# One weight-conversion chunk per unit in the second and third expert blocks, and two operand differences made separately

## The chip, the cores and the metric

The kernel runs on one core of a Trainium2 chip. The metric is device time in microseconds (us) of one execution. The core has a matrix engine (TensorE, "PE" in the profile, with its weight loads shown apart as "PEld"), a vector engine (VectorE, "DVE"), a scalar engine (ScalarE, "ACT"), a further elementwise engine (GpSimd, "POOL") and a sync engine (SyncE, "SP") whose queue issues every DMA of this kernel. Each engine carries out its own instructions in the order in which the program wrote them; semaphores hold an instruction back until what it reads has been written and what it overwrites has been read.

## What is computed

Three stages follow each other, all in float32. The first is windowed attention over 4 batches, 8 heads, 576 positions and 64 dimensions a head. The second routes its 2304 token rows of 512 values through all eight experts and mixes the results with a matrix `P` that is balanced by eight rounds of row and column normalisation. The third is a feed-forward layer with a cosine in it, whose two weight matrices arrive as float64 and are turned into float32 on the chip.

```python
x = attention(q, k, v)                      # (2304, 512)
for e in range(8):
    h = np.maximum(x @ w1[e], 0.0)          # (2304, 1024)
    out += P[:, e:e + 1] * (h @ w2[e])      # (2304, 512)
h = out @ w_in                              # w_in, w_out: float64
return ((h * np.cos(h)) @ w_out).astype(np.float32)
```

## The kernel before, in words

**Blocks and units.** After attention the 2304 token rows are handled as three blocks of 768 rows. The outer list `phases` is expert block 0, 1, 2 (`("moe", b)`), then feed-forward block 0, 1, 2 (`("ffn", b)`). Inside a block the kernel walks over units; a unit is a slice of 256 hidden columns. An expert block has 32 units (8 experts of 4 slices), a feed-forward block has 8, so there are 120 units. Below, "unit 8 of expert block 1" means `u == 8` there.

**The first product, `g1`.** The hidden slice (256 columns by 768 rows, split two by two) is made with seven products of half size in place of eight, in the order `ORDER = (1, 2, 6, 5, 7, 4, 3)`. Their right-hand operands are `B11, B21, T2, T1, T3, T4, B22`: three are quarters of the block's input `src`, and four are differences, `T1 = b12 - b11`, `T2 = b22 - T1`, `T3 = b22 - b12`, `T4 = b21 - T2`. Every operand is split into a rounded high part and a rest, so each product is six matmuls (L750), 42 in a unit. ACT copies partial results out of PSUM (`keep`, L773), DVE adds (L776), and ACT and DVE make the split of the ReLU (L711, L712).

**The second product, `g2`.** For each of six groups of 128 rows, six matmuls (L846 to L848) multiply the hidden slice with the second weight; DVE scales and adds the result (L837; L827 in the feed-forward blocks). The groups of a unit are carried out during the next unit, in an expert block one after each of its products two to seven, so that a unit has 42 + 36 = 78 matmuls.

**Slots and background lists.** After each product, and again after each `g2` group, the main loop calls `slot()`, which lets the first generator of each of the lists `pre`, `feed`, `bg` and `bg2` run on to its next `yield`. An expert unit therefore has 7 + 6 = 13 slots. The order in which instructions are written there is the order in which the engines take them.

**Weight conversion.** `convert_f64(c)` is on the list `bg`. It turns one of 32 chunks (128 by 512 values) of the float64 weights into float32 with seven DVE instructions (L218 to L238), one to a slot; in its eighth slot it issues the load of the next chunk's raw words (`load_f64`, L203 or L209, 512 KB, into the only tile `u0`), and in its tenth the 256 KB store of its own result (L246). The load has to wait until L234 has read the raw words of the chunk before. The result tile `fb` is single too: L230 of the next chunk waits until the store has landed. All 32 generators are appended at once, after unit 0 of expert block 1, so that a new chunk starts in the eleventh slot after the one before.

**Other background work.** `prep_ffn` (list `bg2`) starts after every fifth unit of expert blocks 1 and 2, eight times in all: it loads four converted chunks (L88), makes four differences on POOL (L120), splits eleven pieces on ACT and POOL (L179, L181) and stores them (L175). The weights of the coming units are loaded by `load_w` (L109): 1792 KB for the first product (`wa`), issued at the start of a unit, and 1024 KB for the second (`wb`), issued after the last `g2` group, when the tile that it overwrites has been read. All of these loads and stores go through SP in program order.

**Change of block.** Four units before the end of a block, `feed` starts making the next block's differences: `stages` writes `T1` and `T2` on POOL (L267); for a feed-forward block `x2_pieces` first transposes the expert result. In the last unit `combos` splits one operand after each product from the second on (ACT L284, then DVE L285). `T3` and `T4` have no tiles of their own: `T3` is written over `T1` and `T4` over `T2`, both by the callback `st["rest"]`, which runs after the split of `T1`. The tiles of `T1` and `T2` come from `u_pool` for the expert blocks and feed-forward block 0, and from `rawp` for feed-forward blocks 1 and 2. `rawp` has two buffers for each tag.

Of the kernel before, what the change touches and what calls it, by code (L numbers as in the profile page):

```python
# [29 lines left out]
def tile_attention_moe_cos_ffn(ctx, tc, q, k, v, w_gate, w1, w2, w_in, w_out, out):  # L30
# [9 lines left out]
    NU1 = E * UPE  # L40
    NU2 = DFF // FU
# [29 lines left out]
    with tc.manual_schedule():  # L71
# [123 lines left out]
        def load_f64(c):  # L195
            if c >= 4 * NU2:
                return
            s, x = divmod(c, 4)
            raw = u_pool.tile([P, 512, 2], I32, tag="u0", name=f"f64_{c}")
            if x < 2:  # L200
                for y in range(2):
                    kc = 2 * x + y
                    nc.sync.dma_start(  # L203
                        out=raw[:, y * FU:(y + 1) * FU, :].rearrange("p n t -> p (n t)"),
                        in_=w_in[kc * P:(kc + 1) * P, 2 * s * FU:2 * (s + 1) * FU],
                    )
            else:
                r0 = s * FU + (x - 2) * P
                nc.sync.dma_start(out=raw.rearrange("p n t -> p (n t)"), in_=w_out[r0:r0 + P, :])  # L209
            f64_t[c] = raw  # L210

        def convert_f64(c):
            raw = f64_t.pop(c)
            lo, hi = raw[:, :, 0], raw[:, :, 1]
            a = u_pool.tile([P, 512], I32, tag="u1", name=f"fa{c}")
            b = u_pool.tile([P, 512], I32, tag="u2", name=f"fb{c}")
            w = b.bitcast(F32)
            nc.vector.tensor_scalar(  # L218
                out=a, in0=hi, scalar1=20, scalar2=0x7FF, op0=ALU.logical_shift_right, op1=ALU.bitwise_and
            )  # L220
            yield
            nc.vector.tensor_scalar(out=a, in0=a, scalar1=896.0, scalar2=896.0, op0=ALU.max, op1=ALU.subtract)
            yield
            nc.vector.tensor_scalar(out=a, in0=a, scalar1=23, scalar2=None, op0=ALU.logical_shift_left)
            yield
            nc.vector.scalar_tensor_tensor(
                out=a, in0=hi, scalar=-2147483648, in1=a, op0=ALU.bitwise_and, op1=ALU.bitwise_or
            )
            yield
            nc.vector.tensor_scalar(  # L230
                out=b, in0=hi, scalar1=0xFFFFF, scalar2=0x100000, op0=ALU.bitwise_and, op1=ALU.bitwise_or
            )
            yield
            nc.vector.scalar_tensor_tensor(  # L234
                out=w, in0=lo.bitcast(U32), scalar=2.0 ** -32, in1=b, op0=ALU.mult, op1=ALU.add
            )
            yield
            nc.vector.scalar_tensor_tensor(  # L238
                out=w, in0=w, scalar=2.0 ** -20, in1=a.bitcast(F32), op0=ALU.mult, op1=ALU.mult
            )  # L240
            yield
            load_f64(c + 1)
            yield
            yield
            w32[c] = dram.tile([P, 512], F32, tag=f"w32_{c}", name=f"w32_{c}")
            nc.sync.dma_start(out=w32[c], in_=w)  # L246
# [6 lines left out]
        def stages(b, src):  # L253
            b11, b12 = src[:, 0:2, :HB], src[:, 0:2, HB:]
            b21, b22 = src[:, 2:4, :HB], src[:, 2:4, HB:]
            st = {}
            stg[b] = st

            def stage(nm, i, x, y, over=None):
                if over:  # L260
                    t = st[over]
                elif b in (("ffn", 1), ("ffn", 2)):
                    t = rawp.tile([P, 4, P, 2], F32, tag=("ra", "rb")[i], name=f"st{nm}_{b[0]}{b[1]}")
                    t = t.rearrange("p a f c -> p (a f c)")[:, :TB].rearrange("p (k f) -> p k f", k=2)
                else:
                    t = u_pool.tile([P, 2, HB], F32, tag=("u1", "u2")[i], name=f"st{nm}_{b[0]}{b[1]}")
                nc.gpsimd.tensor_tensor(out=t, in0=x, in1=y, op=ALU.subtract)  # L267
                st[nm] = t

            stage("T1", 0, b12, b11)  # L270
            yield
            yield
            stage("T2", 1, b22, st["T1"])
            st["rest"] = lambda: (stage("T3", 0, b22, b12, "T1"), stage("T4", 1, b21, st["T2"], "T2"))
            yield

        def combos(b, src):
            st = stg[b]
            b11, b21, b22 = src[:, 0:2, :HB], src[:, 2:4, :HB], src[:, 2:4, HB:]
            for nm in ("B11", "B21", "T2", "T1", "T3", "T4", "B22"):  # L280
                s = {"B11": b11, "B21": b21, "B22": b22}.get(nm)
                s = st[nm] if s is None else s
                t = xtp.tile([P, 2, 2, HB], F32R, tag=f"xt{nm}", name=f"xt{nm}_{b[0]}{b[1]}")
                nc.scalar.activation(out=t[:, 0], in_=s, func=AF.Copy)  # L284
                nc.vector.tensor_tensor(out=t[:, 1], in0=s, in1=t[:, 0].bitcast(F32), op=ALU.subtract)  # L285
                xt[b, nm] = t
                if nm == "T1":
                    st["rest"]()
                yield


# [310 lines left out]
        for n in range(NGR + 6):  # L602
            if n < NGR:
                pi, u = groups[n]
# [35 lines left out]
            if n == 46:  # L640
                early.append(stages(("moe", 0), xr[0]))
            if n == 54:
                early.append(combos(("moe", 0), xr[0]))
# [37 lines left out]
        bg, bg2, pre, feed = [], [], [], []  # L681

        def step_all(lst):
            if lst and next(lst[0], StopIteration) is StopIteration:
                lst.pop(0)

        def lazy(f):
            yield from f()

        def slot():  # L690
            step_all(pre)
            step_all(feed)
            step_all(bg)
            step_all(bg2)
# [163 lines left out]
        def begin(n):  # L858
            if n < len(steps):
                kind, b, u = steps[n]  # L860
                if b or kind == "ffn":
                    load_w(u, b, "a")
                elif u >= 2:
                    pre.append(prep_a(u))
            if n + 1 < len(steps):
                kind, b, u = steps[n + 1]
                if not b and kind == "moe" and u >= 3:
                    pre.append(prep_s(u))
# [10 lines left out]
        def tick():  # L879
            tail[:] = [t for t in tail if next(t, StopIteration) is not StopIteration]  # L880

        bg.append(sinkhorn((p_m, "m"), skp))
        load_f64(0)
        queue = []
        for n, s in enumerate(steps):
            kind, b, u = s
            pre += pre_next
            pre_next.clear()
            begin(n + 1)
            ph = phases.index((kind, b))  # L890
            last = n + 1 == len(steps) or steps[n + 1][:2] != (kind, b)
            nxt = phases[ph + 1] if ph + 1 < len(phases) else None
            to_end = (NU1 if kind == "moe" else NU1 + NU2) - u
            if nxt and to_end == 4:
                if nxt[0] == "ffn":
                    feed.append(x2_pieces(nxt[1]))
                    feed.append(lazy(lambda nxt=nxt: stages(nxt, x2r[nxt[1]])))
                else:
                    feed.append(stages(nxt, xr[nxt[1]]))
            nx = None  # L900
            if last and nxt:
                while feed:
                    step_all(feed)
                nx = combos(nxt, xr[nxt[1]] if nxt[0] == "moe" else x2r[nxt[1]])
            for j, _ in enumerate(g1(s)):
                tick()
                slot()
                if queue and (queue[0][0] < n - 1 or j >= (1 if steps[queue[0][0]][0] == "moe" else 6)):
                    m, tt = queue.pop(0)
                    g2(steps[m], tt)  # L910
                    if tt == TPB - 1:
                        begin_b(m + 2)
                    slot()
                tick()
                if nx and j >= 1:
                    next(nx, None)
            if nx:
                for _ in nx:
                    pass
            queue += [(n, tt) for tt in range(TPB)]  # L920
            if (kind, b) == ("moe", 1) and u == 0:
                bg += [convert_f64(c) for c in range(4 * NU2)]
            at = n - NU1
            if 0 < at <= 5 * NU2 and at % 5 == 0:
                bg2.append(prep_ffn(NU1 + at // 5 - 1))
            while pre:
                step_all(pre)
# [34 lines left out]
```

## Time and profile before

| what | value |
|---|---|
| median of three runs | 2156.83 us (2154.12 to 2157.45) |
| the profiled execution's own time | 2155.78 us |
| its span, first to last instruction | 2154.0 us |
| PE busy | 2084.9 us, 97% |
| DVE busy | 1351.5 us, 63% |
| ACT busy | 771.0 us, 36% |
| POOL busy | 470.1 us, 22% |
| moved by DMA | 456.95 MB, 212 GB/s in the mean |

An engine's busy time is the sum of the stretches in which it carried out an instruction. A matmul's end is modelled and matmuls overlap each other, so the 97% of PE does not say that it works at its peak; what a unit takes from its first matmul to the next unit's first is the better measure. In the answers about groups and in the order of time, a text in square brackets tells how long the engine stood idle before an instruction and which event ended that.

### The profile page before, as it was taken

The numbers are of one execution on the slowest core, as the hardware profiler recorded it, in microseconds if no ns is written. First come the engines' busy times: TensorE is split into PE (matmuls) and PEld (weight loads), VectorE is DVE, ScalarE is ACT, GpSimd is POOL, SyncE is SP. The second block draws the span as 40 slices with busy tenths as digits, with TensorE's granted clock in tenths as the row PEclk, the third lists the DMA queues.
The fourth block names the chain that finished last, engine by engine and source line by source line (L and its number), as shares of the span: only waits on it lengthen the run. The fifth ranks groups of instructions, "written<-read, shape, count | busy, mean of one in ns | idle before, by whom it ended". The sixth has DMA issues, their size and how long they took to land. (4 is left out here: it accounts for less than half of the span.)

```text
span 2154.0 us, 28332 instructions
## 1 busy us (share of the span) xinstructions
PE 2084.9 (97%) x10623; PEld 1816.9 (84%) x10623; DVE 1351.5 (63%) x2473; ACT 771.0 (36%) x1544; POOL 470.1 (22%) x524
## 2 busy tenths in 40 slices
PE   8989999999999989999999999999999999999998
PEld 6667888988888878777878888888989888888897
DVE  5665766666666667766775554545555466766766
ACT  6775333333333212222222232222222245454543
POOL 4343232333332001112112121110000012222222
PEclk9999999999999999999999999999999999999999
DMA  5633566676767567777786566574544444454543
GB/s 144 158 104 93 185 256 257 249 263 238 264 235 265 205 239 274 259 254 277 258 288 244 213 226 246 212 265 162 201 175 186 190 175 182 161 209 194 194 166 117
DMA packets 162105, 456.95 MB, mean 212 GB/s; under 512 B 67504, under 2 KB 106416, under 8 KB 131248
## 3 DMA queue, kind: packets, MB, share of 16 engines
q1 hardware_dynamic: 161968, 455.15, 58.3%
q8 instruction: 83, 1.36, 0.3%
q14 instruction: 54, 0.44, 0.1%
HBM read 326.65 MB, written 128.45 MB: 211 GB/s over the span
## 5 line engine op out<-in xcount | busy, mean ns | idle before, releaser
L837 DVE SCALAR_TENSOR_TENSOR acc_moe<-g_moe,prob,acc_moe 128x512 f32<-128x512 f32 x546 | 407.8, 747 | 259.3 <-PE g_moe L848 258.5
L846 PE MATMUL g_moe<-wb,h_moe 128*128 128x512 f32 x1152 | 451.9, 392 | 18.4 <-ACT h_moe L711 18.1
L848 PE MATMUL g_moe<-wb,h_moe 128*128 128x512 f32 x1152 | 461.0, 400 | 5.3 <-DVE h_moe L712 5.2
L847 PE MATMUL g_moe<-wb,h_moe 128*128 128x512 f32 x1152 | 456.2, 396 | 0.0
L773 ACT ACTIVATE s_moe<-y_moe 128x384 f32<-128x384 f32 x288 | 141.3, 491 | 682.2 <-PE y_moe L750 682.1
L750 PE MATMUL y_moe<-xtT_moe,wa 128*128 128x384 f32 x1728 | 349.8, 337 | 0.6 <-ACT s_moe L773 0.6
L750 PEld LDWEIGHTS y_moe<-xtT_moe,wa 128*128 128x128 f32 x1728 | 310.5, 189 | 26.4 <-ACT s_moe L773 0.9
L848 PEld LDWEIGHTS g_moe<-wb,h_moe 128*128 128x128 f32 x1152 | 216.6, 188 | 60.4 <-DVE h_moe L712 15.0
L711 ACT ACTIVATE h_moe<-c_moe 128x384 fp32r<-128x384 f32 x192 | 131.7, 686 | 378.7 <-DVE c_moe L776 378.7
L846 PEld LDWEIGHTS g_moe<-wb,h_moe 128*128 128x128 f32 x1152 | 217.4, 189 | 50.4 <-ACT h_moe L711 24.1
L847 PEld LDWEIGHTS g_moe<-wb,h_moe 128*128 128x128 f32 x1152 | 216.7, 188 | 27.1
L712 DVE SCALAR_TENSOR_TENSOR h_moe<-c_moe,h_moe 128x384 fp32r<-128x384 f32 x192 | 146.5, 763 | 144.5 <-ACT h_moe L711 144.5
L120 POOL TENSOR_TENSOR s<-ra 128x256 f32<-128x256 f32 x80 | 59.5, 743 | 717.0 <-DMA ra<-w 401.8
L776 DVE TENSOR_TENSOR c_moe<-z_moe,s_moe 128x384 f32<-128x384 f32 x192 | 106.6, 555 | 75.0 <-ACT s_moe L773 63.9
L738 POOL TENSOR_TENSOR h_ffn<-c_ffn,h_ffn 128x768 fp32r<-128x768 f32 x48 | 89.1, 1859 | 285.6 <-ACT h_ffn L736 220.2
L750 PE MATMUL z_moe<-xtB_moe,wa 128*128 128x384 f32 x576 | 119.1, 342 | 11.5 <-DVE c_moe L776 11.5
L750 PEld LDWEIGHTS z_moe<-xtB_moe,wa 128*128 128x128 f32 x576 | 103.5, 191 | 23.9 <-DVE c_moe L776 16.5
L750 PE MATMUL y_moe<-xtB_moe,wa 128*128 128x384 f32 x576 | 116.1, 336 | 0.0
L750 PE MATMUL z_moe<-xtT_moe,wa 128*128 128x384 f32 x576 | 115.9, 335 | 0.0
L750 PE MATMUL x_moe<-xtB_moe,wa 128*128 128x384 f32 x576 | 115.6, 335 | 0.0
L846 PE MATMUL g_ffn<-wb,h_ffn 128*128 128x512 f32 x288 | 113.0, 392 | 2.3 <-DVE acc_ffn L827 2.3
L827 DVE TENSOR_TENSOR acc_ffn<-g_ffn,acc_ffn 128x512 f32<-128x512 f32 x126 | 86.4, 687 | 44.7 <-PE g_ffn L848 43.4
(159 smaller groups left out, 3072.0 us busy)
## 6 DMA issues: line engine op xcount, KB each, us to landing
wa<-wd SPq DMA_DIRECT2D x88, 1792.0 KB, 9.1
wb<-wd SPq DMA_DIRECT2D x88, 1024.0 KB, 4.8
wd<-wa SPq DMA_DIRECT2D x32, 1792.0 KB, 6.8
wd<-wb SPq DMA_DIRECT2D x32, 1024.0 KB, 5.3
ra<-in_moe_w_dram SPq DMA_DIRECT2D x64, 256.0 KB, 7.4
rb<-in_moe_w_dram SPq DMA_DIRECT2D x64, 256.0 KB, 5.7
wd<-hla SPq DMA_DIRECT2D x48, 256.0 KB, 9.6
wd<-hlb SPq DMA_DIRECT2D x40, 256.0 KB, 7.4
```

What stands on the lines that cost most here:

```text
L120: nc.gpsimd.tensor_tensor(out=s4[:, o], in0=x, in1=y, op=op)
L711: nc.scalar.activation(out=h[:, 0, cols], in_=c, func=AF.Relu)
L712: nc.vector.scalar_tensor_tensor(out=h[:, 1, cols], in0=c, scalar=0.0, in1=h[:, 0, cols].bitcast(F32), op0=ALU.max, op1=ALU.subtract,)
L738: nc.gpsimd.tensor_tensor(out=h[:, 1], in0=c, in1=h[:, 0].bitcast(F32), op=ALU.subtract)
L750: nc.tensor.matmul(ps[:, :HB], wa[:, wl, WI[m], kc, :], x[:, xl, kc, :], start=start and kc == 0 and n_ == 0, stop=stop and kc == 1 and n_ ...
L773: nc.scalar.activation(out=snap[i], in_=y[:, :HB], func=AF.Copy)
L776: nc.vector.tensor_tensor(out=o, in0=ps[:, :HB], in1=snap[i], op=ALU.add)
L827: nc.vector.tensor_tensor(out=a, in0=ps, in1=a, op=ALU.add)
L837: nc.vector.scalar_tensor_tensor(out=a, in0=ps, scalar=pe, in1=a, op0=ALU.mult, op1=ALU.add)
L846: nc.tensor.matmul(ps, hf[f][:, 0, ts], wb[:, 0, f, :], start=f == 0, stop=False)
L847: nc.tensor.matmul(ps, hf[f][:, 0, ts], wb[:, 1, f, :], start=False, stop=False)
L848: nc.tensor.matmul(ps, hf[f][:, 1, ts], wb[:, 0, f, :], start=False, stop=f == 1)
```

## The change

It has three edits. In the first, an expert unit appends at most one conversion chunk to `bg`, at its end: units 0 to 26 of expert block 1, then the units of expert block 2 until all 32 chunks are appended. In the second, `stages` of all three feed-forward blocks takes its tiles from `rawp`, and `T3` and `T4` get the second buffer of each tag, so that POOL writes all four differences from `feed` without waiting for a split. In the third, for the expert blocks, where `T3` and `T4` still overwrite `T1` and `T2`, each is written as soon as the split of the tile that it overwrites has been issued: `T4` after that of `T2`, `T3` after that of `T1`.

```diff
-                elif b in (("ffn", 1), ("ffn", 2)):
+                elif b[0] == "ffn":
                     t = rawp.tile([P, 4, P, 2], F32, tag=("ra", "rb")[i], name=f"st{nm}_{b[0]}{b[1]}")
...
             stage("T2", 1, b22, st["T1"])
-            st["rest"] = lambda: (stage("T3", 0, b22, b12, "T1"), stage("T4", 1, b21, st["T2"], "T2"))
-            yield
+            yield
+            if b[0] == "ffn":
+                yield
+                stage("T3", 0, b22, b12)
+                yield
+                yield
+                stage("T4", 1, b21, st["T2"])
+                yield
+            else:
+                st["after"] = {"T2": lambda: stage("T4", 1, b21, st["T2"], "T2"),
+                               "T1": lambda: stage("T3", 0, b22, b12, "T1")}
...
                 xt[b, nm] = t
-                if nm == "T1":
-                    st["rest"]()
+                if nm in st.get("after", ()):
+                    st["after"][nm]()
                 yield
...
+        chunk = 0
...
-            if (kind, b) == ("moe", 1) and u == 0:
-                bg += [convert_f64(c) for c in range(4 * NU2)]
+            if chunk < 4 * NU2 and ((kind, b) == ("moe", 1) and u < NU1 - 5 or (kind, b) == ("moe", 2)):
+                bg.append(convert_f64(chunk))
+                chunk += 1
```

## The prediction

> **What bounds the kernel now.** I read the page first, for the engine that sets the time.
>
> ```profile
> PE 2084.9 (97%) x10623; PEld 1816.9 (84%) x10623; DVE 1351.5 (63%) x2473; ACT 771.0 (36%) x1544; POOL 470.1 (22%) x524
> ```
>
> PE leads by far, so the change is worth what it takes from PE's lost time. I then split the span at each unit's first matmul. Columns: stretch, its length, then each engine's busy time with its instructions in brackets, the granted clock, DMA share, GB/s.
>
> ```profile
> 689.13:708.61 19.48, 17.75 (x80) 15.35 (x78) 11.80 (x16) 5.87 (x10) 1.50 (x1) 0.91 0.44 175
> 708.61:739.89 31.28, 31.28 (x158) 28.11 (x156) 23.81 (x42) 6.08 (x12) 0.00 (x0) 1.00 0.62 236
> 739.89:1143.19 403.30, 375.31 (x1795) 324.15 (x1794) 279.69 (x483) 87.16 (x183) 52.94 (x60) 0.99 0.72 261
> 1143.19:1237.03 93.84, 93.84 (x469) 84.34 (x468) 52.02 (x75) 26.15 (x52) 20.13 (x22) 1.00 0.64 238
> 1237.03:1257.82 20.79, 17.76 (x79) 15.35 (x78) 12.33 (x16) 7.35 (x14) 7.26 (x7) 0.92 0.52 190
> 1745.35:1763.32 17.97, 16.18 (x80) 13.93 (x78) 10.79 (x14) 5.73 (x9) 1.56 (x1) 1.00 0.41 162
> 1873.05:1891.09 18.04, 16.29 (x79) 13.90 (x78) 13.68 (x19) 10.03 (x14) 6.54 (x4) 1.00 0.40 151
> ```
>
> A unit has 78 matmuls. The fourth row holds six units (469 matmuls) in 93.84 us: an undisturbed unit takes 93.84 / 6 = 15.64 us. The second row, units 1 and 2 of expert block 1, is as fast (31.28 / 2). The third row, units 3 to 25, holds 23 units (1795 / 78) and takes 403.30 us where 23 x 15.64 = 359.72 would do: **43.6 us are lost there**. The first, fifth and sixth rows are the first units of expert blocks 1 and 2 and of feed-forward block 0; they lose 3.8, 5.2 and 2.3 us. The last is the first unit of feed-forward block 1, which loses 2.4 us; I take block 2's to be alike.
>
> Units 1 to 25 are those in which chunks are converted. Who waits in the lossy stretch is told by the waits between 739.89 and 1143.19 us (total, times, longest):
>
> ```profile
> DVE fa L218 <- DMA f<-in_moe_w_in_dram: 31.8, 9, 6.7
> DVE fa L218 <- DMA f<-in_moe_w_out_dram: 21.1, 7, 8.8
> DVE fb L230 <- DMA w<-fb: 18.9, 6, 4.3
> PE g_moe L846 <- ACT h_moe L711: 12.2, 10, 2.2
> PE z_moe L750 <- DVE c_moe L776: 11.5, 10, 4.2
> PE g_moe L848 <- DVE h_moe L712: 4.0, 15, 0.3
> ```
>
> PE waits for the sums and ReLUs of DVE and ACT, never for a transfer. DVE stands still for 71.8 us, waiting for the raw words of the next chunk (L218) or for the store of the last one (L230). Everything behind that instruction on DVE stands too: the evictions L837, the sums L776 that free PSUM for PE, the ReLU rests L712. So the loss comes from late transfers, handed on by DVE. In units 1 and 2 DVE carried some 17 conversion instructions (42, against 2 x 12.5 by the fourth row), waited for no transfer, and PE lost nothing, which is why I do not blame the instructions.
>
> **The change, part by part. First edit, the chunks.** A chunk takes ten slots, a unit has thirteen. Before, chunks drift through the unit, and the load (eighth slot) is only three slots ahead of the L218 that needs it. After, chunk c runs in slots 1 to 10 of one unit, the load in slot 8 is six slots ahead, and all seven DVE instructions lie in slots 1 to 7, ahead of the sum after the fifth product. The number of instructions and bytes stays the same. Is six slots enough? Unit 1 has the new alignment already, since chunk 0 starts in its slot 1; units 6 and 8 show the transfers beside preparation work. Rows of DVE and of SP in order of time (start, length), and unit 8 as a stretch:
>
> ```profile
> 710.42 0.42 DVE L218 TENSOR_SCALAR fa<-f 128x512 int32<-128x512 int32 x1
> 722.68 0.42 DVE L218 TENSOR_SCALAR fa<-f 128x512 int32<-128x512 int32 x1
> 806.49 0.43 DVE L218 TENSOR_SCALAR fa<-f 128x512 int32<-128x512 int32 x1 [8.79 <-DMA f<-in_moe_w_out_dram]
> 845.07 0.43 DVE L218 TENSOR_SCALAR fa<-f 128x512 int32<-128x512 int32 x1 [0.52 <-DMA f<-in_moe_w_out_dram]
> ...
> 716.55 0.81 SPq L203 DMA_DIRECT2D f<-in_moe_w_in_dram  x2
> 791.03 0.32 SPq L109 DMA_DIRECT2D wb<-wd  x1
> 791.40 0.43 SPq L109 DMA_DIRECT2D wa<-wd  x1
> 791.88 1.22 SPq L88 DMA_DIRECT2D ra<-w  x2
> 794.55 0.33 SPq L209 DMA_DIRECT2D f<-in_moe_w_out_dram  x1
> 838.91 0.34 SPq L209 DMA_DIRECT2D f<-in_moe_w_out_dram  x1
> ...
> 829.10:846.10 17.00, 16.23 (x80) 13.96 (x79) 13.56 (x24) 4.44 (x10) 4.24 (x4) 1.00 0.96 337
> ```
>
> In the new alignment L218 comes 710.42 - 708.61 = 1.8 us into its unit, so the raw words have until 15.64 + 1.8 = 17.4 us after the start of the unit that loads them. In unit 1 the load went out at 7.9 us and had landed before 14.1 us (L218 at 722.68 did not wait): at least 3.3 us to spare. Where the preparation puts its four loads ahead of it, the words landed at 806.49, 15.5 us after the `wb` row at 791.03 that marks the unit's start: 1.9 us to spare. In unit 8, with the preparation's stores and DMA at a share of 0.96, they landed at 845.07, 16.0 us after the unit's start at 829.1: 1.4 us to spare. I take no wait in most units and a residual of 1.5 us in all; the bounds are 0 and, if the units beside preparation (by its yields 45 of every 65 slots, two thirds) kept half their loss, 43.6 x 0.67 x 0.5 = 14.6 us. The store goes out behind the load and has five slots more, so L230 is covered wherever L218 is. Behind the load on SP stand only stores: L234 (slot 6) has run by slot 8, and `wb` and `wa` come at the unit's edge. The five chunks moved to expert block 2 run beside the same work with the same room; I cost them at nothing, and at 5 x 0.6 = 3 us (14.6 us over 23 units) if that cover is gone. Term: -43.6 + 1.5 = **-42.1 us**.
>
> **Second edit, feed-forward blocks.** Rows at the start of feed-forward block 0 (POOL, ACT, DVE) and block 1 (ACT, DVE, and PE's wait from 1856 to 1891 us):
>
> ```profile
> 1743.25 1.85 POOL L267 TENSOR_TENSOR stT_ffn<-x2r 128x768 f32<-128x768 f32 x1 [47.18 <-DVE xtT_ffn L285]
> 1745.05 1.86 POOL L267 TENSOR_TENSOR stT_ffn<-x2r,stT_ffn 128x768 f32<-128x768 f32 x1
> 1745.13 0.85 ACT L284 ACTIVATE xtT_ffn<-stT_ffn 128x768 fp32r<-128x768 f32 x1 [2.92 <-POOL stT_ffn L267]
> 1742.16 0.95 DVE L285 TENSOR_TENSOR xtT_ffn<-stT_ffn,xtT_ffn 128x768 fp32r<-128x768 f32 x1
> 1746.01 1.72 DVE L285 TENSOR_TENSOR xtT_ffn<-stT_ffn,xtT_ffn 128x768 fp32r<-128x768 f32 x1 [1.77 <-ACT xtT_ffn L284]
> 1747.65 0.55 DVE L776 TENSOR_TENSOR c_moe<-z_moe,s_moe 128x384 f32<-128x384 f32 x1
> ...
> 1873.87 0.85 ACT L284 ACTIVATE xtT_ffn<-stT_ffn 128x768 fp32r<-128x768 f32 x1 [3.54 <-POOL stT_ffn L267]
> 1876.38 0.55 DVE L776 TENSOR_TENSOR c_ffn<-z_ffn,s_ffn 128x384 f32<-128x384 f32 x1
> 1882.82 0.84 ACT L730 ACTIVATE ta<-ta 128x768 f32<-128x768 f32 x1 [2.95 <-DVE ta L727]
> ...
> PE y_ffn L750 <- ACT s_ffn L773: 1.9, 3, 1.1
> ```
>
> POOL's T3 waits for the split of T1; ACT then waits 2.92 us for T3, DVE 1.77 us for ACT, and the unit's last sum L776, which the ReLU and the first `g2` group need, stands behind them on DVE until 1747.65. With T3 made long before, its split follows T1's at 1743.1 and L776 comes about 3 us sooner. That is more than the 2.3 us lost: **-2.3 us**. In block 1 ACT stands 3.54 us for T3, and all that follows on ACT and DVE is as late, down to the cosine chain's L730 at 1882.82, behind which `keep` waits, and PE for it: 1.9 us, 1.1 the longest. DVE's evictions are paced by PE, so not all of the lead reaches L730; I take it to remove the 1.1 us wait and most of the rest, 1.7 of the 2.4 us: **-3.4 us** for blocks 1 and 2 together. Bounds: -2.3 - 2 x 2.4 = -7.1, and +1.9, one 1.85 us POOL operation in the way of DVE in mid-block, since T1 to T4 may now run back to back there. I stay near the waits.
>
> **Third edit, expert blocks.** T4 leaves the stretch beside T3's split: DVE's 1.72 us there against 0.95 alone falls away, 0.8 us. But T4 now runs on POOL right after T2's split, and rows of that place in block 1's change say what it meets:
>
> ```profile
> 682.70 0.95 DVE L285 TENSOR_TENSOR xtT_moe<-stT_moe,xtT_moe 128x768 fp32r<-128x768 f32 x1
> 684.81 0.56 DVE L712 SCALAR_TENSOR_TENSOR h_moe<-c_moe,h_moe 128x384 fp32r<-128x384 f32 x1 [0.59 <-ACT h_moe L711]
> ...
> 1234.78 1.45 POOL L120 TENSOR_TENSOR s<-ra,s 128x256 f32<-128x256 f32 x1
> 1236.20 1.85 POOL L267 TENSOR_TENSOR stT_moe<-xr 128x768 f32<-128x768 f32 x1
> ```
>
> T4 would run from 683.65 to 685.50 and L712 would start at 684.81 in its middle. The 1.72 us fits a full stop: T4 ended at 1746.91, 0.90 after that split began, and 0.90 + 0.95 is close to it. Then L712 and the T1 split behind it are 0.7 us later, and T3 with them: gain 0.8, price 0.7, **0** for block 1. In block 2 POOL was busy with L120 until T3 at 1236.20; T4 pushes in ahead of two L120s and T3, 1.85 us, against about 1 us of relief: **+0.8 us**. Bounds for both: -1.6 (the relief, unpaid) and +3.7 (1.85 each).
>
> [...]
>
> The sum: -42.1 - 2.3 - 3.4 + 0 + 0.8 = -47.0 us. The profiled execution took 2155.78 us, 1.05 below the median of the runs, so it gives 2108.8 us; I say **2109 us**, 2.2% faster.
>
> **The rivals.**
> (a) *The raw words are still late beside preparation.* For: only 1.4 to 1.9 us to spare there. Against: the waits before came where the load had three slots, not six. At the upper bound of the residual it gives 2109 + 14.6 - 1.5 = 2122 us.
> (b) *The boundary edits give nothing*, since POOL's differences only move their conflicts with DVE: 2155.8 - 42.1 + 0.8 = 2114 us.
> (c) *The conversion instructions themselves cost PE.* Then 32 chunks cost what 32 did, and only the boundaries gain: 2155.8 - 4.9 = 2151 us. Against: 31.28 us for the two units of the second row.
> (d) *Slower: a fixed alignment repeats a fixed stall.* If words landed late in the loading unit every time, each of the 32 chunks would stall DVE at the same place, with nothing drifting out of it. It decides once the landing passes 17.4 us by over 1.5 us (48 / 32). At 3 us late a unit loses some 3 us: 32 x 3 = 96, against 47 gained: 2205 us. Against: landings of at most 14.1 to 16.0 us.
> (e) *More than the sum:* the clock comes back too. The granted clock reads 0.91 and 0.92 at the first units of expert blocks 1 and 2, 19.48 x 0.09 = 1.8 and 20.79 x 0.08 = 1.7 us. Shorter waits may spare both, the residual may be nought, and the feed-forward starts may lose nothing (2 x 0.7): 2109 - 3.5 - 1.5 - 1.4 = 2103 us. [...]
>
> **How the numbers follow.** Forecast 0.55 (2105 to 2112), (a) 0.13, (b) 0.13, (c) 0.04, (d) 0.03, (e) 0.12. From 2101, below (e), to 2122, (a), it holds all but (c), (d) and the outer parts of (a) and (e), some 15%. A measurement of this kernel tells 0.2%, 4.3 us, from no change. Forecast, (a), (b) and (e) are faster, 0.93, and (c) at 2151 is by a hair; unforeseen mishaps included I say 0.94 faster, 0.03 same, 0.03 slower.
>
> **What would show it.** Right: L218 and L230 no longer wait for DMA, and units 3 to 25 of expert block 1 take 15.64 us; the first ones of the feed-forward blocks show no ACT wait for POOL; block 2 of the experts still loses about 5 to 6 us. Wrong: L218 waiting in units beside L88 or L175 speaks for (a), units above 15.64 us without a DVE wait for (c), the same wait in every unit for (d).

## The result, and the profile after

The changed kernel takes 2108.61 us (median of four runs, 2106.59 to 2109.7); the kernel before, run beside it, 2157.14 us (four runs, 2154.12 to 2162.32). The ratio is 0.977, with a 95% interval of 0.9753 to 0.9787. The profiled execution took 2106.59 us with a span of 2104.8 us.

The page's line of the engines, for the changed kernel:

```profile
PE 2072.0 (98%) x10623; PEld 1819.4 (86%) x10623; DVE 1355.9 (64%) x2473; ACT 774.1 (37%) x1544; POOL 467.5 (22%) x524
```

The instructions are the same in number as before, on every engine. The span fell by 49.2 us with hardly a change in the busy time of any engine but PE. PE's idle time fell by 36.3 us (2154.0 - 2084.9 before, 2104.8 - 2072.0 now), its busy time by 12.9 us for the same instructions. So the gain is time in which PE had waited or had run slowly. The stretches show where. Each begins and ends at a unit's first matmul: units 1 to 31 of expert block 1, the first units of expert blocks 1 and 2, units 1 to 5 of expert block 2, the first units of feed-forward blocks 0, 1 and 2, and the last unit with the end of the program (start and end, length, busy time of PE, PEld, DVE, ACT and POOL with their instructions, clock, DMA share, GB/s):

```profile
707.42:1192.26 484.84, 484.84 (x2419) 435.79 (x2418) 344.37 (x564) 123.22 (x246) 68.65 (x81) 1.00 0.74 272
688.07:707.42 19.35, 17.75 (x79) 15.35 (x78) 11.05 (x16) 6.13 (x10) 0.32 (x1) 0.91 0.45 175
1192.26:1214.06 21.80, 17.61 (x79) 15.00 (x78) 11.59 (x16) 7.35 (x14) 6.92 (x9) 0.92 0.49 182
1214.06:1292.26 78.20, 78.20 (x391) 70.29 (x390) 57.13 (x95) 20.06 (x42) 11.97 (x15) 1.00 0.76 279
1701.59:1717.23 15.64, 15.64 (x79) 14.06 (x78) 8.81 (x13) 5.11 (x8) 0.00 (x0) 1.00 0.47 186
1826.99:1842.63 15.64, 15.64 (x79) 14.05 (x78) 11.98 (x18) 7.18 (x11) 3.98 (x2) 1.00 0.43 156
1956.54:1972.18 15.64, 15.64 (x80) 14.06 (x79) 11.97 (x18) 7.19 (x11) 3.98 (x2) 1.00 0.42 155
2066.02:2104.80 38.78, 32.67 (x145) 27.35 (x143) 24.25 (x33) 11.21 (x15) 7.33 (x4) 0.94 0.21 76
```

The same stretches of the kernel before that the prediction did not show: units 1 to 31 of expert block 1 as one, the first unit of feed-forward block 2, and the end:

```profile
708.61:1237.03 528.42, 500.43 (x2419) 436.61 (x2418) 355.52 (x599) 119.39 (x246) 73.07 (x82) 0.99 0.70 256
2004.97:2023.01 18.04, 16.31 (x79) 13.89 (x78) 13.69 (x19) 10.03 (x14) 6.54 (x4) 1.00 0.40 148
2116.85:2154.00 37.15, 31.07 (x145) 26.18 (x143) 24.26 (x33) 11.21 (x15) 7.33 (x4) 1.00 0.21 80
```

In the changed kernel 31 units take 484.84 us, which is 31 x 15.64: nothing is lost there, though units 1 to 27 convert a chunk each; nor is anything in the fourth row (78.20 / 5), the units of block 2 that convert the other five. Before, the same units took 528.42 us, 43.6 us more. The three feed-forward starts are at 15.64 us too (before 17.97, 18.04 and 18.04). The starts of the expert blocks still lose, 19.35 and 21.80 us against 19.48 and 20.79, and the end is 1.6 us longer, at a clock of 0.94 against 1.00.

Does DVE still wait for the raw words, or for the store? The answers about the lines L218 and L230 in the changed kernel, all 32 conversions (duration shortest, median, longest in ns; then what its engine waited for, in the same words for both):

```profile
L218 DVE TENSOR_SCALAR fa<-f x32: 414/416/419, 709.2 to 1278.4; 128x512 int32<-128x512 int32 x32
...
L230 DVE TENSOR_SCALAR fb<-f x32: 415/417/595, 714.2 to 1283.4; 128x512 int32<-128x512 int32 x32
its engine sat idle before it (us, times) until:
```

Nothing follows the last line in either answer: no DMA wait is left. The margin is thin in one place. In unit 11 of block 1, beside the preparation's four loads, this row of SP, and then the row of the DMA issues in that unit (count, KB, median us to landing), give the latest landing:

```profile
871.77 0.33 SPq L209 DMA_DIRECT2D f<-in_moe_w_out_dram  x1
```

```profile
f<-in_moe_w_out_dram SPq DMA_DIRECT2D x1, 512.0 KB, 8.3
```

The unit's first matmul began at 707.42 + 10 x 15.64 = 863.8 us. The load went out 8.0 us later and landed 8.3 us after that, 16.3 us into the unit; the L218 that needs it stands at 17.4.

### The profile page after: what moved, and what is told of

It reads as the page before. It is cut to its first block, busy times and chain, and to the rows that moved or that the text cites. A ratio compares the mean times of both kernels' runs of the same rounds, so it can differ in the third digit from the quotient of the medians.

```text
span 2104.8 us, 28340 instructions
## 1 busy us (share of the span) xinstructions
PE 2072.0 (98%) x10623; PEld 1819.4 (86%) x10623; DVE 1355.9 (64%) x2473; ACT 774.1 (37%) x1544; POOL 467.5 (22%) x524
## 4 chain that ended last, share of the span: by engine, by line
PE 93%; DVE 3%; ACT 1%; POOL 1%; issue 1%; DMA 0%; SPq 0%; ACTq 0%; POOLq 0%; DVEq 0%
PE y_moe L759 18%; PE g_moe L857 13%; PE g_moe L856 12%; PE g_moe L855 12%; PE z_moe L759 9%; PE x_moe L759 4%; PE y_ffn L759 4%; PE g_ffn L857 3%; PE g_ffn L856 3%; PE g_ffn L855 3%; PE s L443 3%; PE z_ffn L759 2%; PE x L535 2%; PE x_ffn L759 1%; PE T L407 1%
## 5 line engine op out<-in xcount | busy, mean ns | idle before, releaser
L721 DVE SCALAR_TENSOR_TENSOR h_moe<-c_moe,h_moe 128x384 fp32r<-128x384 f32 x192 | 148.8, 775 | 144.4 <-ACT h_moe L720 144.4
L855 PE MATMUL g_ffn<-wb,h_ffn 128*128 128x512 f32 x288 | 113.5, 394 | 2.3 <-DVE acc_ffn L836 2.3
L857 PE MATMUL g_ffn<-wb,h_ffn 128*128 128x512 f32 x288 | 114.7, 398 | 0.0
```

What stands on the lines that cost most here:

```text
L721: nc.vector.scalar_tensor_tensor(out=h[:, 1, cols], in0=c, scalar=0.0, in1=h[:, 0, cols].bitcast(F32), op0=ALU.max, op1=ALU.subtract,)
L855: nc.tensor.matmul(ps, hf[f][:, 0, ts], wb[:, 0, f, :], start=f == 0, stop=False)
L857: nc.tensor.matmul(ps, hf[f][:, 1, ts], wb[:, 0, f, :], start=False, stop=f == 1)
```

## The experiments

A stretch "loses" what it takes over 15.64 us a unit; "the stretch" is units 1 to 31 of expert block 1, whose undisturbed length is 484.84 us. Ratios are to the kernel before, timed on the same chip in the same rounds.

**First edit alone.** The kernel before, with only the list of conversions changed.

```diff
-            if (kind, b) == ("moe", 1) and u == 0:
-                bg += [convert_f64(c) for c in range(4 * NU2)]
+            if chunk < 4 * NU2 and ((kind, b) == ("moe", 1) and u < NU1 - 5 or (kind, b) == ("moe", 2)):
+                bg.append(convert_f64(chunk))
+                chunk += 1
```

> Only the first edit. Late-transfer theory (the loss was DVE standing for raw words and stores that came too late): units 3 to 25 of expert block 1 take 15.64 us each, 43.6 us are won, the block starts lose what they lost before (3.8, 5.2, 2.3, 2.4, 2.4 us), about 2113.5 us in all. Instruction theory (the conversion's DVE instructions crowd out PE's helpers, wherever they stand): 32 chunks cost what 32 cost, 2157 us, with the loss now spread over units 1 to 27.

Measured: 2114.23 us, ratio 0.9801 (0.9775 to 0.9827). Its stretch, and the first units of expert block 2 and of feed-forward block 0:

```profile
710.40:1195.24 484.84, 484.84 (x2419) 435.79 (x2418) 344.02 (x564) 123.02 (x246) 68.23 (x82) 1.00 0.73 272
1195.24:1216.12 20.88, 17.75 (x79) 15.37 (x78) 12.32 (x16) 7.36 (x14) 7.36 (x7) 0.92 0.52 190
1703.65:1721.64 17.99, 16.20 (x80) 13.95 (x78) 10.79 (x14) 5.73 (x9) 1.56 (x1) 1.00 0.42 162
```

All 43.6 us of the stretch come from this edit, and the starts stay as they were (20.79 and 17.97 before).

**Second edit alone.** The kernel before, with the feed-forward blocks' differences in tiles of `rawp`; the expert blocks keep `st["rest"]`.

```diff
-                elif b in (("ffn", 1), ("ffn", 2)):
+                elif b[0] == "ffn":
...
+            if b[0] == "ffn":
+                yield
+                stage("T3", 0, b22, b12)
+                yield
+                yield
+                stage("T4", 1, b21, st["T2"])
...
```

> Only the second edit. If the differences' own tiles are what removed the losses at the three feed-forward block starts (2.3 + 2.4 + 2.4 us), about 2150 us, with 15.64 us in each of the three first units; the conversion stretch still takes some 403 us. If those gains came from the calmer transfers of the first edit, 2157 us.

Measured: 2153.36 us (ten runs), ratio 0.9972 (0.9959 to 0.9984). Its stretch and the first unit of feed-forward block 0 (those of blocks 1 and 2 take 15.64 us as well):

```profile
708.53:1235.69 527.16, 501.51 (x2420) 437.82 (x2418) 354.98 (x599) 119.29 (x246) 71.08 (x82) 0.99 0.70 256
1745.25:1760.89 15.64, 15.64 (x79) 14.05 (x78) 8.82 (x13) 5.11 (x8) 0.00 (x0) 1.00 0.47 186
```

The edit takes all that the three starts had lost, 2.3 + 2.4 + 2.4 = 7.1 us; the medians (2158.94 us before in these rounds) differ by 5.6. The stretch still loses 42.3 us.

**Without the third edit.** The changed kernel, with the expert blocks' `T3` and `T4` written together after the split of `T1`, as before.

```diff
-                st["after"] = {"T2": lambda: stage("T4", 1, b21, st["T2"], "T2"),
-                               "T1": lambda: stage("T3", 0, b22, b12, "T1")}
+                st["rest"] = lambda: (stage("T3", 0, b22, b12, "T1"), stage("T4", 1, b21, st["T2"], "T2"))
```

> First and second edit, without the third: T3 and T4 of the expert blocks both after T1's split again. From the traces the third edit cost 1.0 us at expert block 2 and won 0.1 at block 1, so this should be 0.9 us faster than the changed kernel, about 2107.7 us, with 20.8 us in the first unit of expert block 2 and 19.5 in that of block 1. If the place of T4 is not what made block 2's start longer, both starts stay at 21.8 and 19.4.

Measured: 2108.12 us (2105.82 to 2109.99), ratio 0.9771 (0.975 to 0.9793). The first units of expert blocks 1 and 2:

```profile
688.45:706.38 17.93, 16.20 (x79) 13.93 (x78) 11.81 (x16) 5.86 (x10) 1.50 (x1) 1.00 0.48 188
1191.22:1211.96 20.74, 17.64 (x79) 15.05 (x78) 12.32 (x16) 7.35 (x14) 7.46 (x7) 0.92 0.52 191
```

The total can't be told from the changed kernel's. At block 2 the start is 1.1 us shorter without the edit (21.80 with it). At block 1 it is 1.4 us shorter, but the clock reads 1.00 here and 0.91 there, which the last section takes up. A further kernel with the edit, the one with the load in the twelfth slot below, takes 17.78 us there at a clock of 1.00, so the 1.4 us is not the edit's doing.

**Less room for the raw words.** The changed kernel with the store in the eighth slot and the load moved behind it, to the twelfth slot of the unit in one kernel and to the thirteenth, the last, in another, so that the words come late.

```diff
-            load_f64(c + 1)
-            yield
-            yield
             w32[c] = dram.tile([P, 512], F32, tag=f"w32_{c}", name=f"w32_{c}")
             nc.sync.dma_start(out=w32[c], in_=w)
+            for _ in range(4):        # 5 in the second kernel
+                yield
+            load_f64(c + 1)
```

> The changed kernel with the store in slot 8 and the load of the next raw words in slot 12 in place of 8, the last one ahead of the load of wb. If only the landing counts: it goes out some 14 us into the unit to an empty queue and lands 3.4 to 5 us later, at 17.4 to 19 us, against the 17.4 us at which L218 wants it: DVE waits up to 1.5 us in some units, 2109 to 2130 us.

> As the one before, but with the load in slot 13, one slot later and now behind the load of wb on SP, which is let go only at the unit's end. If the order on SP's queue is what makes a load late: it lands behind 1024 KB (4.8 us), at about 15.64 + 4.8 + 1.7 = 22 us, L218 waits some 4.7 us in every converting unit, PE loses 2 to 3 us in each of 32, and the time is 2170 to 2205 us, slower than before (the slower rival of the prediction). If DVE's slack within a unit takes up such a wait, 2109 to 2130 us.

Measured, twelfth slot: 2106.87 us, ratio 0.9774 (0.9756 to 0.9791), the same as the changed kernel. Its stretch; then the store of unit 8 of block 1 and the load behind it, with the last conversion instruction on DVE:

```profile
705.23:1190.07 484.84, 484.84 (x2419) 435.79 (x2418) 346.23 (x563) 123.26 (x246) 68.80 (x81) 1.00 0.76 272
```

```profile
839.56 0.68 DVE L238 SCALAR_TENSOR_TENSOR fb<-fb,fa 128x512 f32<-128x512 f32 x1
840.27 0.33 SPq L243 DMA_DIRECT2D w<-fb  x1
840.69 1.71 SPq L203 DMA_DIRECT2D f<-in_moe_w_in_dram  x2
```

The unit's first matmul began at 705.23 + 8 x 15.64 = 830.35. The load went out 10.3 us later, not at the 14 us that I had worked out from its slot. A slot orders the instructions of one engine; SP issued the load right behind the store, and the store when L238 had written its tile (839.56 + 0.68 = 840.24). So this run did not make the words late, and told nothing of lateness.

Measured, thirteenth slot: 2117.77 us, ratio 0.9822 (0.9806 to 0.9839); one of its four runs took 4102.66 us where the others took 2116.63 to 2118.0, for a reason that is not known, and the ratio leaves it out. The stretch; the waits of DVE (total, times, longest); and rows of one unit, whose first matmul began at 773.77:

```profile
710.82:1201.09 490.27, 489.35 (x2419) 434.20 (x2418) 328.50 (x564) 117.69 (x246) 69.48 (x80) 1.00 0.72 269
```

```profile
DVE fa L218 <- DMA f<-in_moe_w_in_dram: 55.1, 15, 4.9
DVE fa L218 <- DMA f<-in_moe_w_out_dram: 49.4, 15, 3.7
```

```profile
780.42 0.43 DVE L218 TENSOR_SCALAR fa<-f 128x512 int32<-128x512 int32 x1 [3.74 <-DMA f<-in_moe_w_in_dram]
...
786.27 0.55 DVE L785 TENSOR_TENSOR c_moe<-z_moe,s_moe 128x384 f32<-128x384 f32 x1
786.87 1.00 PEld L759 LDWEIGHTS z_moe<-xtB_moe,wa 128*128 128x128 f32 x6 [0.17 <-DVE c_moe L785]
```

Here the words were late for 30 of the 32 chunks, and DVE stood for 55.1 + 49.4 = 104.5 us, more than the 71.8 us of before. By the reasoning of the prediction the time should have been 2170 us or more; it came out as the expectation's other case has it, in which DVE's slack takes up the wait. The stretch lost 490.27 - 484.84 = 5.4 us. The rows tell why: the wait ends 6.7 us into the unit, and PE waits for nothing of DVE before the sum after the fifth product, at 786.27. In between DVE makes up what it is behind. It has room for that: 344.37 / 31 = 11.1 us of work in a unit of 15.64. PE's weight load behind that sum waited 0.17 us for it.

So my reason was too short. It is not the wait as such that costs; I formed a second theory: **what a late transfer costs depends on the place in the unit at which DVE stands still, and it costs most just before the sum that frees PE's accumulator (`z`) for the unit's last product.** Two further runs put the seven conversion instructions at that place.

**The late place, with late words and with early ones.** The changed kernel with six empty slots ahead of the first chunk's L218 (so that all conversions lie in slots 7 to 13). In the first kernel the load goes out in slot 6 of the unit that needs it; in the second right behind the seventh instruction, six slots sooner.

```diff
             w = b.bitcast(F32)
+            for _ in range(6 if c in (0, NU1 - 5) else 0):
+                yield
...
             yield
-            load_f64(c + 1)
-            yield
-            yield
             w32[c] = dram.tile([P, 512], F32, tag=f"w32_{c}", name=f"w32_{c}")
             nc.sync.dma_start(out=w32[c], in_=w)
+            for _ in range(5):
+                yield
+            load_f64(c + 1)
```

The second kernel has the same first part, and behind the seventh instruction:

```diff
-            yield
             load_f64(c + 1)
-            yield
             yield
             w32[c] = dram.tile([P, 512], F32, tag=f"w32_{c}", name=f"w32_{c}")
             nc.sync.dma_start(out=w32[c], in_=w)
+            for _ in range(5):
+                yield
```

> The changed kernel with each chunk's seven DVE instructions moved from slots 1 to 7 to slots 7 to 13 (six empty slots ahead of chunks 0 and 27) and the next raw words loaded in slot 6, just ahead of the L218 that needs them. The words then land behind wb and wa at 12 to 16 us, and L218 wants them at about 8 us: some 4 us of waiting in each of 32 units, like the run with the load in slot 13 (104.5 us in 30 waits, 5.8 us lost), but now ahead of the sum after the fifth product. If it is the sum of DVE's waits that counts, about 2115 to 2120 us. If it is their place in the unit, 2 to 3 us are lost in each of 32 units: 2150 us or more, as slow as the kernel before or slower.

> The same late place of the seven instructions, but the next raw words are loaded in slot 13, as soon as L234 has read the last ones; they stand behind wb alone and land about 6.5 us into the next unit, ahead of the 8 us at which L218 comes. No waits. If the waits' place is what counts, this stays within 6 us of the changed kernel: 2108 to 2115 us. If the late place of the instructions themselves costs PE, 2130 us or more.

Measured, late words: 2177.2 us, ratio **1.0082** (1.0067 to 1.0097), slower than before. Its stretch and units 1 to 7 of expert block 2; its waits for raw words; what PE waited for in the stretch; and rows around the L220 (the same instruction as L218, two lines down) of a unit with one of the longest waits, in order of time:

```profile
709.34:1251.23 541.89, 505.29 (x2419) 437.88 (x2418) 336.10 (x564) 117.87 (x246) 71.14 (x81) 0.99 0.65 243
1273.39:1393.71 120.32, 113.28 (x548) 99.16 (x546) 71.75 (x119) 28.00 (x60) 18.39 (x21) 0.99 0.67 245
```

```profile
DVE fa L220 <- DMA f<-in_moe_w_out_dram: 48.6, 15, 5.9
DVE fa L220 <- DMA f<-in_moe_w_in_dram: 42.0, 15, 6.0
```

```profile
PE g_moe L857 <- ACT h_moe L722: 18.0, 17, 1.6
PE z_moe L761 <- DVE c_moe L787: 13.6, 9, 3.0
```

```profile
897.23 0.65 DVE L220 TENSOR_SCALAR fa<-f 128x512 int32<-128x512 int32 x1 [5.89 <-DMA f<-in_moe_w_out_dram]
897.80 0.54 DVE L787 TENSOR_TENSOR c_moe<-z_moe,s_moe 128x384 f32<-128x384 f32 x1
...
898.40 1.33 PE L761 MATMUL z_moe<-xtB_moe,wa 128*128 128x384 f32 x6 [2.98 <-DVE c_moe L787]
```

Measured, early words: 2117.51 us, ratio 0.9808 (0.9792 to 0.9825). Its stretch:

```profile
705.55:1200.09 494.54, 489.43 (x2419) 436.09 (x2418) 337.68 (x563) 123.09 (x246) 77.33 (x81) 1.00 0.76 266
```

With 90.6 us of DVE waits ahead of the sum (L787 follows the wait at once, and PE's product, or the ReLU and the group that reads it, follows L787), the stretch loses 541.89 - 484.84 = 57.1 us and block 2's seven units 120.32 - 109.48 = 10.8 us: 67.9 in all, three quarters of the wait, against a twentieth at the early place (5.4 of 104.5). PE's two waits make 31.6 of the 57.1 us; most of the rest is in its busy time, 505.29 us against 484.84. With the same place and early words it loses 9.7 us. So 47.4 of the 57.1 us are the words', and 9.7 the place's own. The 9.7 us is more than expected: if only the waits' place counted, the early kernel should have stayed at 2115 us or below.

**Fewer loads at the old place.** The kernel before with its drifting chunks and three slots of room, of whose 32 raw loads only the first is carried out; the others' words are left out, and each chunk converts the first one's.

```diff
+            if c:
+                f64_t[c] = f64_t["one"]
+                return
             s, x = divmod(c, 4)
-            raw = u_pool.tile([P, 512, 2], I32, tag="u0", name=f"f64_{c}")
+            raw = f64_t["one"] = u_pool.tile([P, 512, 2], I32, tag="u0", name=f"f64_{c}")
```

> The kernel before with its 1.3 chunks a unit, but only the first chunk's raw words are loaded and every chunk converts these (the other 31 loads are left out, so the feed-forward weights repeat one chunk). Late-transfer theory: the 52.9 us of L218's waits are gone, only the stores' waits at L230 (18.9 us) remain, and of the 43.6 us lost in units 3 to 25 at most 15 stay: 2126 us or less. Instruction theory: DVE carries as many instructions as before, so the loss stays at about 43 us and the time at 2155 us.

Measured: 2123.92 us (two runs), ratio 0.9853 (0.9833 to 0.9872). Its stretch; then the one DMA wait of DVE that is left:

```profile
711.76:1203.54 491.78, 488.63 (x2420) 434.81 (x2419) 358.20 (x599) 121.75 (x246) 73.62 (x82) 1.00 0.66 242
```

```profile
DVE fb L233 <- DMA w<-fb: 14.1, 6, 4.1
```

DVE carries before's instructions (599) at before's places, and the loss falls from 43.6 to 6.9 us, with 14.1 us of waits for the store left. The loads it leaves out also relieve the other transfers (in the stretch a DMA share of 0.66 and 242 GB/s, before 0.70 and 256), so this bounds the waits' share from above: up to 36.7 of the 43.6 us.

**More work for DVE.** The changed kernel with three further 128 by 512 instructions for each chunk, in slots 8 to 10, whose result changes nothing.

```diff
             load_f64(c + 1)
-            yield
-            yield
+            for k in range(3):
+                nc.vector.scalar_tensor_tensor(
+                    out=a, in0=a, scalar=-2147483648, in1=a, op0=ALU.bitwise_and, op1=ALU.bitwise_or
+                )
+                if k < 2:
+                    yield
```

> The changed kernel with three more DVE instructions in each chunk, in slots 8 to 10, of the kind of L226 (about 0.7 us each; they write a scratch tile that is done with). A unit then carries 7 x 0.58 + 2.1 = 6.1 us of conversion on DVE, more than the 5.3 us of the kernel before. Late-transfer theory: no transfer is later, so within 5 us of 2108.6 us. Instruction theory: more than the kernel before lost, 2155 us or above.

Measured: 2113.62 us, ratio 0.9804 (0.9787 to 0.9821). Its stretch:

```profile
709.13:1199.04 489.91, 488.12 (x2419) 434.87 (x2418) 394.02 (x644) 121.65 (x246) 74.01 (x81) 1.00 0.73 269
```

DVE is busy for 394.02 us, 38.5 more than before's 355.52, and the stretch loses 5.1 us where before's lost 43.6. DVE's load is not what made the kernel before slow.

**A tile of its own for `T3`.** What the starts of the expert blocks still lose goes with a wait for POOL (6.04 us of ACT's at block 2, in rows further below), which writes `T3` over `T1` and so must wait for its split. In this kernel `T3` takes the tile `u0` of the raw words, ahead of the splits; the two raw loads that would be in its way move to the end of their blocks.

```diff
-                    t = u_pool.tile([P, 2, HB], F32, tag=("u1", "u2")[i], name=f"st{nm}_{b[0]}{b[1]}")
+                    t = u_pool.tile([P, 2, HB], F32, tag=("u1", "u2", "u0")[i], name=f"st{nm}_{b[0]}{b[1]}")
...
+                stage("T3", 2, b22, b12)
-                st["after"] = {"T2": lambda: stage("T4", 1, b21, st["T2"], "T2"),
-                               "T1": lambda: stage("T3", 0, b22, b12, "T1")}
+                st["after"] = {"T2": lambda: stage("T4", 1, b21, st["T2"], "T2")}
...
-            load_f64(c + 1)
+            if c + 1 != NU1 - 5:
+                load_f64(c + 1)
...
-        load_f64(0)
...
+            if last and kind == "moe" and b < 2:
+                load_f64(chunk)
```

> All three edits, but in the expert blocks T3 gets a tile of its own (that of the raw words, which stands empty at a block's change once the two chunk loads beside it are moved to the block's end) and is written ahead of the last unit like T1 and T2; T4 still goes over T2 after T2's split. If the starts of expert blocks 1 and 2 lose their 3.7 and 6.2 us because ACT and DVE stand for POOL's T3, both come down to 15.64 us and the time to about 2098.7 us. If DVE and POOL getting in each other's way is what sets them, part of the loss stays: 2102 to 2108 us.

Measured: 2097.89 us (2097.42 to 2099.17), ratio **0.9725** (0.9705 to 0.9745), below the interval of the changed kernel. The first units of expert blocks 1 and 2:

```profile
687.65:703.65 16.00, 15.93 (x79) 14.00 (x78) 10.48 (x16) 5.29 (x9) 0.00 (x0) 1.00 0.63 247
1188.49:1205.40 16.91, 16.16 (x79) 13.93 (x78) 11.87 (x16) 6.59 (x13) 6.39 (x8) 1.00 0.75 265
```

The two starts fall by 3.4 and 4.9 us, and the clock reads 1.00 in both; 0.4 and 1.3 us over 15.64 stay, and what holds them was not looked into. That is 8.2 of the 10.7 us between the medians of this kernel and the changed one; the rest is within what the time ahead of the expert blocks varies by (below). This version is the fastest of all.

## Why the prediction was right

**The bound and the place of the loss.** Right. PE's time was lost in the units that convert, and with L218 and L230 no longer waiting for DMA those units take 15.64 us.

**First edit, -42.1 us.** Measured -43.6: the residual of 1.5 us for units beside preparation is 0.0, although the latest landing was 16.3 us into its unit, a little later than the 16.0 reckoned with. The size was right and the reason half of it. The prediction gave the load's six slots as what removes the loss, and named the place of the seven DVE instructions without a price. The runs price both:

| load | place of the conversion | DVE's waits for raw words | lost in the stretch |
|---|---|---|---|
| three slots ahead (before) | drifting | 52.9 us, and 18.9 for the store | 43.6 us |
| one load in all | drifting | none, 14.1 for the store | 6.9 us |
| late | slots 1 to 7 | 104.5 us | 5.4 us |
| late | slots 7 to 13 | 90.6 us | 57.1 us |
| early | slots 7 to 13 | none, 0.5 for the store | 9.7 us |
| early (the change) | slots 1 to 7 | none | 0.0 us |

(The waits of the two late kernels are those of the whole run, their losses those of the stretch.) Early words alone win some 34 to 37 of the 43.6 us, the early place alone some 38, and the two are not added: either breaks the chain from the late transfer over DVE to PE. Both together win it all. The change makes both. It also lowers the rate, from 1.3 chunks a unit to one; that alone is not what wins, since the fourth row has one chunk a unit as well.

**Second edit, -2.3 and -3.4 us.** Measured -2.3 and -4.8. The mis-sized term is the 1.7 of 2.4 us for each of feed-forward blocks 1 and 2: I let part of ACT's lead be eaten by evictions paced by PE, and the whole loss went. The feared bound, a POOL operation in DVE's way in mid-block, did not show: the seven units behind the starts of feed-forward blocks 0 and 1 take 109.76 and 113.91 us, before 109.73 and 113.88.

**Third edit, 0 and +0.8 us.** Measured -0.1 and +1.0 in the two starts. What set them is in these rows of the changed kernel, the first two at the change to block 1, the others at that to block 2:

```profile
682.66 1.86 POOL L267 TENSOR_TENSOR stT_moe<-xr,stT_moe 128x768 f32<-128x768 f32 x1 [5.01 <-DVE xtT_moe L294]
683.74 1.19 DVE L721 SCALAR_TENSOR_TENSOR h_moe<-c_moe,h_moe 128x384 fp32r<-128x384 f32 x1 [0.59 <-ACT h_moe L720]
...
1189.61 2.67 POOL L267 TENSOR_TENSOR stT_moe<-xr,stT_moe 128x768 f32<-128x768 f32 x1
1189.63 0.94 DVE L294 TENSOR_TENSOR xtT_moe<-stT_moe,xtT_moe 128x768 fp32r<-128x768 f32 x1
1195.47 0.84 ACT L293 ACTIVATE xtT_moe<-stT_moe 128x768 fp32r<-128x768 f32 x1 [6.04 <-POOL stT_moe L267]
```

L721 began inside T4's time on POOL (682.66 to 684.52) and took 1.19 us where it took 0.56 before (the prediction's 684.81 row): 0.63 us longer, near the 0.7 reckoned. At block 2 the operation on POOL was the longer one: T4 took 2.67 us against 1.86, with a split on DVE (L294, 0.94 us) begun 0.02 us after it. ACT then stood 6.04 us for T3, the wait that `T3`'s own tile removes.

**What the sum did not hold.** The end took 38.78 us against 37.15, +1.6, at the lower clock. And the first expert unit began at 189.58 us against 190.65, -1.1. Its beginning lies behind attention, which no edit touches, and over the profiles of all these kernels it stood between 187.64 and 192.49 us: chance. The sum of what was measured is -43.6 - 0.1 + 1.0 - 2.3 - 4.8 + 1.6 - 1.1 = -49.3 us, and the spans differ by 49.2. From one profiled execution to the other the prediction was 2.2 us short of the gain (2108.8 against 2106.59); it meets the median, 2108.61, within 0.4 us. That closeness is partly luck: the sum held neither the end nor the beginning, and the two nearly cancel.

**The rivals.** (a), raw words still late beside preparation: no L218 waited; it fell, by a margin of 1.1 us in one unit. (b), boundary edits that give nothing: the second edit alone gives a ratio of 0.9972, with an interval that leaves out 1; it fell. (c), the conversion instructions themselves: 38.5 us more DVE work than before lost 5.1 us; it fell. (d), a fixed stall repeated in every unit: it was not so here, since the words landed in time. Its price, "at 3 us late a unit loses some 3 us", was wrong for the place where the change puts the conversion, where 104.5 us of waits cost 5.4 us in the stretch, and nearer the mark half a unit later, where 90.6 us of waits cost 67.9 and the kernel became slower than before. (e), more than the sum: the clock did not come back, 0.91 and 0.92 at the two starts, but the other two parts of this rival did come, the residual of 0 and the feed-forward starts without loss, 2.9 us by its prices.

## What to carry to other kernels

In these runs a wait cost what stood behind it on its engine at that moment and was needed before the engine could make up for it: 104.5 us of waits cost 5.4 us at the early place, 90.6 us cost 67.9 half a unit later. So background work with a transfer that may be late is best put where its engine has the longest time to its next deadline, and at a fixed place, not one that drifts over all of them; here the early fixed place alone left 5.4 us and early words alone 6.9 to 9.7, so either cures most. And a tile that is overwritten at the change of a block is worth a tile of its own, even one borrowed from work that could move its load: here that won more than hoisting the overwrite.

## What the runs showed of the hardware that was not expected

**The clock read 0.50 for 3.41 us behind a wait of 1.34 us, and 1.00 behind the same wait in another run.** The wait of PE in the first unit of expert block 1 of the changed kernel, and two stretches of 3.41 us, around it and behind it:

```profile
691.66 0.50 PE L855 MATMUL g_moe<-wb,h_moe 128*128 128x512 f32 x1 [1.34 <-ACT h_moe L720]
```

```profile
690.24:693.65 3.41, 1.81 (x7) 1.12 (x7) 2.50 (x5) 2.69 (x4) 0.00 (x0) 1.00 0.97 384
693.65:697.06 3.41, 3.41 (x11) 3.12 (x11) 2.46 (x4) 0.49 (x1) 0.00 (x0) 0.50 0.95 402
```

The clock reads 0.50 in the second stretch. In the kernel with the load in the twelfth slot the same unit holds the same wait and runs at full clock; its row, and the whole unit:

```profile
691.04 0.50 PE L855 MATMUL g_moe<-wb,h_moe 128*128 128x512 f32 x1 [1.34 <-ACT h_moe L720]
```

```profile
687.45:705.23 17.78, 16.17 (x79) 13.93 (x78) 11.05 (x16) 6.13 (x10) 0.32 (x1) 1.00 0.49 188
```

It takes 17.78 us where the changed kernel takes 19.35, and PE is busy for 16.17 us in place of 17.75: 1.6 us for the clock alone. From the first expert unit on, the clock reads 0.50 in four places of the changed kernel's profile and in four of the kernel before's, and in the 3.41 us ahead of each PE had stood idle for 1.60 to 3.29 us. What decides whether the clock halves behind such idle time is not shown here. At half clock for 3.41 us PE loses up to 1.7 us, by my estimate. The end's +1.6 us is of this kind (PE busy for 32.67 us against 31.07, the clock at 0.94 against 1.00), so the whole of it can't be charged to the change. The loss in units 3 to 25 of the kernel before holds 10.2 us at half clock, with PE busy for 8.8 of them: by the same estimate some 4.4 of its 43.6 us, behind waits that the change removes (its stretch reads 1.00). With `T3`'s own tile PE's wait in the first unit of block 2 falls from 4.2 to 0.7 us, and the clock reads 1.00 at both starts.

**SP does not keep to the slots.** A load written into the twelfth slot went out 10.3 us into a unit whose slots last 15.64 us, as the store ahead of it on the queue waited only for L238; only the thirteenth slot, behind the load of `wb`, made it late.
